# The guess for batch 2 taken out of the third attention, and two loads of v moved behind stores, in a kernel of attention and experts

## The chip, the cores and the metric

The kernel runs on one core of a Trainium2 chip, as one launch. The metric is the time of one execution on the device, in microseconds (us). Three runs of the kernel before took 358.21, 357.4 and 357.49 us; the median is 357.49. One further execution was recorded by the hardware profiler; all rows below come from it.

## The reference, cut to what matters

Eight batches; 16 query heads share 4 key heads; 384 tokens of 64 numbers per head. Each token's 16 heads side by side make a row of 1024, which goes to one of 16 experts (4 groups of 4).

```
scores = q @ k.T / sqrt(64);  attn = softmax(scores);  a = attn @ v        # per head
x = a.transpose(0, 2, 1, 3).reshape(3072, 1024)
g = argmax(x @ w_group);  e = argmax(x @ w_expert[g])                      # per token
out = softmax_g[g] * softmax_e[e] * (relu(x @ w1[g, e]) @ w2[g, e])
```

The kernel loads one expert per batch, chosen ahead of the gate by a guess from the mean of v, weights its output by what the gate really says, and has a loop at the end for tokens whose expert was not that one.

## The kernel before, in words

**Attention.** `Attn(b)` handles batch b in 24 units (`NU`), six to each pair of heads. For a unit TensorE makes a score (L318, four bf16 matmuls into a PSUM tile of the kind `s`, of which there are two), ScalarE its exp (L324) into one of 16 `e` tiles, and TensorE multiplies that by v (`pv`, L337, eight float32 matmul records into a tile of the kind `o`, two of them). `run` issues score u+2 ahead of pv u, then the unit's tail and whatever a table (`steps0`, `steps1`, `steps2`) puts there; a key such as 4.5 stands between pv 4 and the tail of unit 4. The sums of the exps are formed in pairs: GpSimd adds unit u to unit u-1 (`pair`, L345), then VectorE reduces the pair (`reduce`, L354). For a unit named in `apart` GpSimd adds nothing, and VectorE reduces both. `later` names units whose pair is called by hand, `lags` the unit at which a reduce is called. `join_keys` adds the parts, `sums` takes the total by four matmuls with a constant (L416) and VectorE's reciprocals (L432).

**Between two attentions.** `normalise` has VectorE spread the reciprocals (L455) and multiplies x by them (L459, on VectorE or GpSimd); `cast` writes x in bf16 (L464 on ScalarE, L466 on GpSimd). The block of batch b then computes the gate of batch b (`gate_logits`, L474, 64 matmul records) and the expert of batch b-1: `moe_h` (`ffn_h`, L636: four tiles of 16 matmuls) and `ffn_y` (L650, three chunks of 16), whose rows ScalarE or VectorE scales (`y_out`) and SP stores by two DMAs a chunk (L671).

**The guess.** The sum of v over the keys (`sum_v`: three GpSimd additions, L112 to L114; for batch 0 one VectorE reduce, L121) is halved and summed over partitions by a matmul of two columns (`guess_mean`, L480), copied by VectorE (L482), and multiplied with the gate's matrix (`guess_logits`, L487). For batch 2 this happens in units 1 and 2 of its own attention, followed by nine small VectorE instructions that pick the expert (`pick_guess`). The gate's tile of batch 1 is the same PSUM tile. For batch 3 the mean stands between the halves of the second chunk of `ffn_y`, for batches 4 to 7 (`ahead`) in front of the first chunk.

**Loads.** SP loads v in float32 (`load_v`, L105, two buffers), transposes k and q by DMA (L152, L153, L147) and stores the output, all in the order in which the code issues them. GpSimd issues the loads of k and q (L96, L101), which write bf16 into one buffer each, and of w1 and w2 (L546, L552), 2 MB each as written; the profile calls the queue of GpSimd's loads q0 and that of SP's DMAs q1. In `first_block` (behind the second attention) `load_v(3)` is issued first; in `block(2)` `load_v(4)`. `after_transposes` makes GpSimd wait until the DMA transposes of q are done (L604) before it fetches the weights. In `block(3)` the order on GpSimd is load_k(5), load_q(5), sum_v(4), that wait, the fetches, and the pairs of the fourth batch's attention.

Everything is issued in the order of the code on each engine; no planner moves it.

Of the kernel before, what the change touches and what calls it, by code (L numbers as in the profile page):

```python
# [10 lines left out]
BF16 = mybir.dt.bfloat16  # L11
# [7 lines left out]
def kernel(  # L19
# [48 lines left out]
    def ps_tile(which, shape=None, dtype=F32):  # L68
        if which == "x":
            which = f"o{1 - turn['o']}"  # L70
        else:
            turn[which] = 1 - turn[which]
            which += str(turn[which])
        return psum.tile(shape or [P, 2, 512], dtype, name="ps_" + which)
# [11 lines left out]
    def head_pair(m):  # L86

        g, r = m // 2, m % 2
        return KG * (2 * (g // 2) + r) + g % 2
# [13 lines left out]
    def load_v(b, src=None):  # L103
        vraw[b] = vpool.tile([P, NA, NC * D], F32, name="v_raw")
        nc.sync.dma_start(out=vraw[b], in_=rows(v[b] if src is None else src))  # L105
# [9 lines left out]
                             in1=s[:, :, 2 * D:])  # L115
        vsum[b] = t

    def first_sum_v():
        vsum[0] = gpool.tile([P, NA * D], BF16, name="vsum")
        with nc.allow_low_precision(reason="the guess of an expert alone reads this"):  # L120
            nc.vector.tensor_reduce(  # L121
                out=vsum[0].rearrange("p (a d) -> p a d", d=D),
                in_=vraw[0].rearrange("p a (c d) -> p a d c", d=D), axis=AX.X, op=ALU.add)

    def new_qT(b):
        qT[b] = xpool.tile([P, KQ * SC, P], BF16, name="qT")
# [282 lines left out]
                in_=red3[b][:, g:h, :parts[b][g]].rearrange("p g c t j -> p g (t j) c"),  # L409
                axis=AX.X, op=ALU.add)  # L410

    def sums(b, g0, g1, which, tiles=False):
        sm = ps_tile(which)[:, :, :(g1 - g0) * 2 * NB]
        for r in range(2):
            if not tiles:
                nc.tensor.matmul(out=sm[:, r], lhsT=half32[:, r, :],  # L416
                                 rhs=red[b][:, g0:g1].rearrange("p g t j -> p (g t j)"),
                                 start=True, stop=True)
                continue
            rs = slice(r * H2, (r + 1) * H2)  # L420
            for t in range(2):
                nc.tensor.matmul(
                    out=sm[t * D:(t + 1) * D, r].rearrange("p (g t j) -> p g t j", t=2, j=NB)[:, :, t],
                    lhsT=half32[rs, r, t * D:(t + 1) * D], rhs=red[b][rs, g0:g1, t],
                    start=True, stop=True)
        if b not in inv:
            inv[b] = gpool.tile([P, KQ, NB], F32, name="inv", bufs=2)
        iv = inv[b][:, 2 * g0:2 * g1].rearrange("p (g r) j -> p r g j", r=2)
        sm = sm.rearrange("p r (g t j) -> p r g t j", t=2, j=NB)
        for t in range(2):  # L430
            ts = slice(t * D, (t + 1) * D)
            nc.vector.reciprocal(out=iv[ts], in_=sm[ts, :, :, t])  # L432

    Q = P // 4

# [25 lines left out]
    def cast(b, m, eng=None):  # L461
        ks = slice(2 * m, 2 * m + 2)
        if eng is None:
            nc.scalar.copy(out=xb[b][:, ks, :], in_=xT[b][:, ks, :])  # L464
        else:
            eng.tensor_copy(out=xb[b][:, ks, :], in_=xT[b][:, ks, :])  # L466
# [3 lines left out]
    def gate_logits(b, pt):  # L470
        for m in range(KQ):
            x = xT[b][:, m, :].rearrange("p (j t x) -> p t j x", t=4, x=32)
            for t in range(4):
                nc.tensor.matmul(out=pt[32 * t:32 * t + 32, 0, :S // 4],  # L474
                                 lhsT=wg[:, head_pair(m), :], rhs=x[:, t],
                                 start=(m == 0), stop=(m == KQ - 1))

    def guess_mean(b, pt):
        pm = pt[:, 1, :2]
        nc.tensor.matmul(out=pm, lhsT=vsum[b], rhs=halfb, start=True, stop=True)  # L480
        vm = gpool.tile([P, 2], BF16, name="vm")
        nc.vector.tensor_copy(out=vm, in_=pm)  # L482
        return vm

    def guess_logits(vm, out_):
        for r in range(2):
            nc.tensor.matmul(out=out_, lhsT=vm[:, r:r + 1].to_broadcast([P, P]),  # L487
                             rhs=wg2[:, r, :], start=(r == 0), stop=(r == 1))
# [142 lines left out]

    def ffn_h(x, w1, hT, f0, which):
        h = ps_tile(which)
        for jj in range(2):
            for m in range(KQ):
                nc.tensor.matmul(out=h[:, jj, :S],  # L636
                                 lhsT=w1[:, head_pair(m), (f0 + jj) * P:(f0 + jj + 1) * P],
                                 rhs=x[:, m, :], start=(m == 0), stop=(m == KQ - 1))
        if f0 + 2 < FQ:
            nc.scalar.activation(hT[:, f0:f0 + 2, :], h[:, :, :S], ACT.Relu)  # L640
        else:
            for jj in range(2):
                nc.scalar.activation(hT[:, f0 + jj, :], h[:, jj, :S], ACT.Relu)  # L643
# [29 lines left out]
    def moe_y(b, c, which):  # L673
        y_out(b, c, ffn_y(w2s[b], hTs[b], c, which))

    def do(f, *a):
        return lambda: f(*a)
# [46 lines left out]
    def x_logits(b):  # L724
# [5 lines left out]
    index_constants()  # L730
    steps0 = {
        0: [gate_matrix_2],
        2: [do(first_q1, "x"), first_sum_v],
        4: [do(first_k, NC, 2 * NC, "x")],
        7: [do(x_mean, 0)],
        8: [do(x_logits, 0)],
# [21 lines left out]
    def first_fetch():  # L758
# [21 lines left out]
            lambda: mean(1, state["pt"]),  # L780
            do(at[1].pair, 7),
            do(at[1].reduce, 7),
            do(moe_h, 0, 2, "s"),
            do(at[1].pair, 13),
            do(at[1].pair, 15),
# [11 lines left out]
    at[1].run(steps1)  # L797

    def first_block():
        load_v(3)  # L800
        moe_y(0, 0, "s")
        sum_v(2)
        load_k(3)
        load_q(3)
        at[1].reduce(NU - 1)
        join_keys(1, 0, Hkv)
        y = ffn_y(w2s[0], hTs[0], 1, "s", (0,))
        sums(1, 0, Hkv, "o")
        ffn_y(w2s[0], hTs[0], 1, "s", (1,), y)
        y_out(0, 1, y)  # L810
        y = ps_tile("o")
        normalise(1, 0, "x")
        normalise(1, 2, "x")
        cast(1, 0)
        ffn_y(w2s[0], hTs[0], 2, "o", (0,), y)
        at[2] = Attn(2, later=(1,), lags={5: [1], 6: [3], **{u: [u - 2] for u in range(7, NU, 2)}})
        at[2].score(0)
        at[2].score(1)
        ffn_y(w2s[0], hTs[0], 2, "o", (1,), y)
        y_out(0, 2, y)  # L820
        normalise(1, 1, None, pool)
        normalise(1, 3, None, pool)

    def second_gate():
        gate_logits(1, state["pt"])
# [2 lines left out]
    first_block()  # L828
    before_attention(2)
    steps2 = {  # L830
        1: [do(cast, 1, 2), do(at[2].pair, 1), do(x_mean, 2)],
        2: [do(x_logits, 2)],
        3: [do(cast, 1, 1)],
        4.5: [second_gate],
        6: [do(cast, 1, 3)],
        8: [do(read_pick, 2)],
    }
    at[2].run(steps2)

# [2 lines left out]
    def block(b):  # L842
        last = b == B - 1
        f = b - 1
        early = b >= EARLY
        if b + 2 < B:
            load_v(b + 2)
        if not early:
            after_transposes(b + 1)
# [15 lines left out]
            pick_w2(b)  # L865
        moe_h(f, 0, "s")
        at[b].reduce(NU - 1)
        join_keys(b, 0, Hkv)
        if b == 2:
            gate_softmax(1, state["gl"], False)()  # L870
            out_weights(1)
# [15 lines left out]
        cast(b, 1)  # L887
        normalise(b, 3)
        moe_y(f, 0, "s")
        cast(b, 2)  # L890
        if not ahead:
            pt = ps_tile("o")
        y = ffn_y(w2s[f], hTs[f], 1, "s", (0,))
        if ahead:
            guess_logits(vm, guess_out(pt))
        elif not last:
            vm = guess_mean(b + 1, pt)
        ffn_y(w2s[f], hTs[f], 1, "s", (1,), y)
        y_out(f, 1, y)
        gate_logits(b, pt)  # L900
        if not (last or ahead):
            guess_logits(vm, guess_out(pt))
        if b <= EARLY:
            at[b + 1] = Attn(b + 1)
            at[b + 1].start()
        cast(b, 3)
        w = gate_softmax(b, gate_rows(pt, not last), not last)
        if not last:
# [165 lines left out]
```

## Time and profile before

| | |
|---|---|
| median of three runs | 357.49 us (357.4 to 358.21) |
| the profiled execution | 356.7 us, of which the instructions span 354.9 |
| TensorE busy | 345.9 us, 97% of the span |
| VectorE, ScalarE, GpSimd busy | 72%, 63%, 62% |
| TensorE's granted clock | 0.996 of full speed over the span |
| DMA | 67.15 MB as written: 41.03 on GpSimd's queue (67.2% of 16 engines), 24.94 on SP's (30.4%) |
| the third attention (batch 2): its unit 0 starts at | 72.98 us |
| the block of batch 2 starts at | 95.04 us |
| the fourth attention (batch 3) starts at | 118.78 us |
| the block of batch 3 starts at | 137.96 us |
| the fifth attention (batch 4) starts at | 160.91 us |

Busy time is read per engine; matmuls are pipelined, so TensorE's is not its work at its peak. A line of the timeline joins neighbouring instructions of one kind, and a bracket at its end says how long the engine stood idle before it and what released it.

### The profile page before, as it was taken

The page shows a single profiled execution, that of the slowest core. Times are in us where ns is not written, and L with a number is a line of the kernel's source. Part 1 is how long each engine was busy: PE and PEld are TensorE (multiplying, and loading weights), DVE is VectorE, ACT ScalarE, POOL GpSimd, SP SyncE. Part 2 cuts the span into 40 slices and gives each one's busy share as a digit, 9 for nine tenths or more (in the row PEclk, how much of TensorE's full clock was granted, in tenths as well). Part 3 has the DMA queues.
Part 4 walks back from the last instruction along what each step waited for, and adds up shares of the span by engine and source line. Part 5 has one row for each costly group of instructions (what it writes and reads, how often), then busy time and mean ns, then how long its engine had stood idle before and what let it go on. Part 6 is the DMA issues. An engine that isn't in the chain of part 4 may idle for free.

```text
span 354.9 us, 9208 instructions
## 1 busy us (share of the span) xinstructions
PE 345.9 (97%) x3801; PEld 182.5 (51%) x3816; DVE 253.9 (72%) x520; ACT 225.0 (63%) x296; POOL 220.2 (62%) x171
## 2 busy tenths in 40 slices
PE   8999999999999999999999999999999999999994
PEld 4455565445555455554555555545545545555642
DVE  5797769767697777976689667886769677796031
ACT  5899925299536795378954499355982669444311
POOL 7889985869935499308991299804995059900000
PEclk9999999999999999999999999999999999999998
DMA  8979999799989999999999999999995995099925
GB/s 199 215 135 188 220 207 160 134 275 222 193 174 176 258 209 182 206 163 203 229 221 207 193 220 211 218 192 193 228 211 95 197 263 130 2 175 219 258 48 137
DMA packets 69327, 67.15 MB, mean 189 GB/s; under 512 B 37113, under 2 KB 49401, under 8 KB 69281
## 3 DMA queue, kind: packets, MB, share of 16 engines
q0 software_dynamic: 26640, 41.03, 67.2%
q1 hardware_dynamic: 42272, 24.94, 30.4%
q8 instruction: 32, 0.52, 0.6%
q10 hardware_dynamic: 368, 0.54, 0.4%
q14 instruction: 15, 0.11, 0.1%
HBM read 86.07 MB, written 12.58 MB: 278 GB/s over the span
## 4 chain that ended last, share of the span: by engine, by line
PE 87%; ACT 4%; POOL 3%; DVE 2%; issue 1%; DMA 1%; ACTq 0%; SPq 0%; POOLq 0%; DVEq 0%
PE ps_o L337 30%; PE ps_s L636 22%; PE ps_s L650 13%; PE ps_s L318 8%; PE ps_o L650 6%; PE ps_o L474 3%; ACT e L324 2%; POOL w L345 2%; PE ps_o L636 1%; PE ps_s L951 1%; PE ps_o L951 1%; DMA w<-in_q_dram 1%; POOL xb L466 1%; ACT w L324 0%; DVE inv L432 0%
## 5 line engine op out<-in xcount | busy, mean ns | idle before, releaser
L345 POOL TENSOR_TENSOR e<-e 128x768 f32<-128x768 f32 x91 | 162.8, 1826 | 37.0 <-PE ps_s L318 30.8
L324 ACT ACTIVATE e<-ps_s 128x768 f32<-128x768 f32 x187 | 147.7, 813 | 15.0 <-PE ps_s L318 12.8
L337 PE MATMUL ps_o<-e,v_raw 64*64 64x384 f32 x1496 | 150.1, 482 | 0.0
L354 DVE TRANSPOSE_TENSOR_REDUCE red<-e 128x24 f32<-128x768 f32 x95 | 91.4, 972 | 36.7 <-POOL e L345 36.6
L636 PE MATMUL ps_s<-xb,w 128*128 128x384 bf16 x480 | 80.1, 326 | 0.1
L337 PEld LDWEIGHTS ps_o<-e,v_raw 64*64 64x64 f32 x1496 | 55.3, 133 | 35.7 <-issue 29.5
L636 PEld LDWEIGHTS <-w 128*128 128x128 bf16 x512 | 49.4, 98 | 36.4 <-issue 4.5
L318 PE MATMUL ps_s<-qT,kT 64*64 64x384 bf16 x768 | 65.0, 325 | 0.4
L650 PEld LDWEIGHTS <-hT 128*128 128x128 bf16 x336 | 31.5, 98 | 37.7 <-issue 1.5
L650 PE MATMUL ps_s<-w,hT 128*128 128x512 bf16 x217 | 49.5, 379 | 0.4
L640 ACT ACTIVATE hT<-ps_s 128x768 bf16<-128x768 f32 x23 | 18.6, 810 | 46.7 <-PE ps_s L636 43.3
L318 PEld LDWEIGHTS <-kT 64*64 64x64 bf16 x768 | 24.5, 105 | 35.6 <-issue 33.6
L669 ACT ACTIVATE ot<-ps_s,we 128x1024 f32<-128x1024 f32 x14 | 15.6, 1115 | 19.0 <-PE ps_s L650 17.2
L604 POOL COPY tok<-qT 1x1 bf16<-1x1 bf16 x6 | 1.1, 179 | 42.5 <-DMA qT<-q_raw 42.5
L379 DVE COPY xT<-ps_o 128x768 f32<-128x768 f32 x26 | 24.0, 924 | 2.7 <-ACT xb L464 1.5
L455 DVE STREAM_TRANSPOSE e<-inv 128x768 f32<-128x768 f32 x26 | 25.2, 971 | 0.2
L464 ACT CAST xb<-xT 128x768 bf16<-128x768 f32 x28 | 23.1, 830 | 3.4 <-DVE xT L459 3.2
L650 PE MATMUL ps_o<-w,hT 128*128 128x512 bf16 x105 | 24.0, 379 | 1.1 <-issue 1.1
L459 DVE TENSOR_TENSOR xT<-xT,e 128x768 f32<-128x768 f32 x24 | 23.1, 962 | 0.8
L495 DVE STREAM_TRANSPOSE gl<-ps_o 128x96 f32<-128x96 f32 x8 | 2.3, 283 | 18.7 <-PE ps_o L474 15.0
L643 ACT ACTIVATE hT<-ps_s 128x384 bf16<-128x384 f32 x14 | 6.1, 488 | 12.5 <-PE ps_o L480 7.2
L474 PEld LDWEIGHTS ps_o<-xT,wg 128*32 128x32 f32 x448 | 9.2, 110 | 3.3 <-issue 2.1
(140 smaller groups left out, 233.3 us busy)
## 6 DMA issues: line engine op xcount, KB each, us to landing
w<-in_moe_w_dram POOLq DMA_DIRECT2D x16, 2048.0 KB, 21.9
out_dram<-ot SPq DMA_DIRECT2D x42, 256.0 KB, 6.9
q_raw<-in_q_dram POOLq DMA_DIRECT2D x7, 768.0 KB, 11.0
v_raw<-in_v_dram SPq DMA_DIRECT2D x7, 384.0 KB, 5.7
k_raw<-in_k_dram POOLq DMA_DIRECT2D x7, 192.0 KB, 6.4
out_dram<-ot SPq DMA_DIRECT2D x10, 128.0 KB, 2.4
w<-in_q_dram POOLq DMA_DIRECT2D x3, 192.0 KB, 6.3
w<-in_k_dram SPq DMA_DIRECT2D x2, 192.0 KB, 3.7
```

The costliest lines, as they stand in the source:

```text
L318: nc.tensor.matmul(out=sT[r * H2:(r + 1) * H2, s, :S], lhsT=kT[b][s * D:(s + 1) * D, key_block(b, s, g // 2, c), ks], rhs=qT[b][s * D:(s + ...
L324: nc.scalar.activation(e.rearrange("p t (s x) -> p s t x", s=2), sT[:, :, :S].rearrange("p s (t x) -> p s t x", t=2), ACT.Exp, scale=scale)
L337: nc.tensor.matmul(out=oT[t * D:(t + 1) * D, r, :S], lhsT=vraw[b][r * H2:(r + 1) * H2, g // 2, c * D:(c + 1) * D], rhs=self.e[u][r * H2:(r ...
L345: nc.gpsimd.tensor_add(out=self.e[u - 1], in0=self.e[u - 1], in1=self.e[u])
L354: nc.vector.tensor_reduce(out=red3[b][:, g, parts[b][g]].rearrange("p t j -> p (t j)"), in_=self.e[w].rearrange("p t (j x) -> p (t j) x", ...
L379: nc.vector.tensor_copy(out=dst, in_=src)
L455: nc.vector.transpose(out=rb.rearrange("p k (j x) -> p k j x", x=32), in_=inv[b][:, ks].unsqueeze(3).to_broadcast([P, 2, NB, 32]))
L459: eng.tensor_mul(out=x, in0=x, in1=rb)
L464: nc.scalar.copy(out=xb[b][:, ks, :], in_=xT[b][:, ks, :])
L474: nc.tensor.matmul(out=pt[32 * t:32 * t + 32, 0, :S // 4], lhsT=wg[:, head_pair(m), :], rhs=x[:, t], start=(m == 0), stop=(m == KQ - 1))
L636: nc.tensor.matmul(out=h[:, jj, :S], lhsT=w1[:, head_pair(m), (f0 + jj) * P:(f0 + jj + 1) * P], rhs=x[:, m, :], start=(m == 0), stop=(m == ...
L650: nc.tensor.matmul(out=y[:, nh, :], lhsT=hT[:, f, c * P:(c + 1) * P], rhs=w2[:, f, nh * HALF:(nh + 1) * HALF], start=(f == 0), stop=(f == ...
```

## The change

- `first_sum_v` becomes `reduce_v(b)`, which also makes the sum of v of batch 2, on VectorE, in the steps at unit 17 of the second attention, behind `reduce(7)`. The three GpSimd additions for batch 2 in `first_block` go.
- The guess of batch 2: its mean is made in `sums(1)` of `first_block`, by one matmul behind those of the sums, into a free part of the same tile, and copied behind the reciprocals. Its logits and the pick stand at unit 1 of the third attention (before: mean at 1, logits at 2).
- In the third attention units 0 and 1 are summed by VectorE (`apart=(1,)`), both reduces at unit 2; `join_keys` of its first heads stands at unit 10.
- The casts of batch 1 (slices 2, 1, 3), before at units 1, 3 and 6, stand together at 4.5, behind the gate of batch 1.
- `load_v(3)` is issued behind `moe_y(0, 0)`, `load_v(4)` behind `moe_y(1, 0)`; each then follows two stores on SP.
- In the block of batch 2 the mean for batch 3 stands behind the gate, its logits behind the first two scores of the next attention.
- `ffn_h` takes its first tile in two passes, first the slices 0 to 5 of x for both halves, then the slices 6 and 7.

```diff
-    def first_sum_v():
+    def reduce_v(b):
...
-    def sums(b, g0, g1, which, tiles=False):
-        sm = ps_tile(which)[:, :, :(g1 - g0) * 2 * NB]
+    def sums(b, g0, g1, which, tiles=False, mean=None):
+        pt = ps_tile(which)
+        sm = pt[:, :, :(g1 - g0) * 2 * NB]
...
+        if mean is not None:
+            guess_product(mean, pt, MEAN)
...
+        return pt if mean is None else guess_copy(pt, MEAN)
...
+    MEAN = 2 * KQ * NB
+
+    def guess_product(b, pt, n):
+        nc.tensor.matmul(out=pt[:, 1, n:n + 2], lhsT=vsum[b], rhs=halfb, start=True, stop=True)
+
+    def guess_copy(pt, n):
+        vm = gpool.tile([P, 2], BF16, name="vm")
+        nc.vector.tensor_copy(out=vm, in_=pt[:, 1, n:n + 2])
+        return vm
...
     def ffn_h(x, w1, hT, f0, which):
         h = ps_tile(which)
-        for jj in range(2):
-            for m in range(KQ):
...
+        ends = [0, KQ] if f0 else [0, KQ - 2, KQ]
+        for m0, m1 in zip(ends, ends[1:]):
+            for jj in range(2):
+                for m in range(m0, m1):
...
             do(at[1].reduce, 7),
+            do(reduce_v, 2),
             do(moe_h, 0, 2, "s"),
...
     def first_block():
+        moe_y(0, 0, "s")
         load_v(3)
-        moe_y(0, 0, "s")
-        sum_v(2)
...
-        sums(1, 0, Hkv, "o")
+        state["vm"] = sums(1, 0, Hkv, "o", mean=2)
...
-        at[2] = Attn(2, later=(1,), lags={5: [1], 6: [3], **{u: [u - 2] for u in range(7, NU, 2)}})
+        at[2] = Attn(2, apart=(1,), lags={6: [3], **{u: [u - 2] for u in range(7, NU, 2)}})
...
     steps2 = {
-        1: [do(cast, 1, 2), do(at[2].pair, 1), do(x_mean, 2)],
-        2: [do(x_logits, 2)],
-        3: [do(cast, 1, 1)],
-        4.5: [second_gate],
-        6: [do(cast, 1, 3)],
+        1: [second_logits],
+        2: [do(at[2].reduce, 1)],
+        4.5: [second_gate, do(cast, 1, 2), do(cast, 1, 1), do(cast, 1, 3)],
         8: [do(read_pick, 2)],
+        10: [do(join_keys, 2, 0, 1)],
     }
...
-        if b + 2 < B:
+        if early and b + 2 < B:
             load_v(b + 2)
...
         moe_y(f, 0, "s")
+        if not early:
+            load_v(b + 2)
         cast(b, 2)
...
-        elif not last:
-            vm = guess_mean(b + 1, pt)
         ffn_y(w2s[f], hTs[f], 1, "s", (1,), y)
         y_out(f, 1, y)
         gate_logits(b, pt)
         if not (last or ahead):
-            guess_logits(vm, guess_out(pt))
+            vm = guess_mean(b + 1, pt)
         if b <= EARLY:
             at[b + 1] = Attn(b + 1)
             at[b + 1].start()
+        if not (last or ahead):
+            guess_logits(vm, guess_out(pt))
```

## Rows read from the trace of the kernel before

**Rows 1.** The page, busy us of each engine (share of the span) and instructions.

```profile
PE 345.9 (97%) x3801; PEld 182.5 (51%) x3816; DVE 253.9 (72%) x520; ACT 225.0 (63%) x296; POOL 220.2 (62%) x171
```

**Rows 2.** Chain of waits, third attention: start us, us, what.

```profile
74.20 0.71 ACT e L324
...
81.64 0.72 ACT xb L464
```

**Rows 3.** Timeline, TensorE, third attention: start us, us, line, operation, tiles, count.

```profile
74.95 0.36 PE L318 MATMUL ps_s<-qT,kT 64*64 64x384 bf16 x4
...
83.12 0.36 PE L318 MATMUL ps_s<-qT,kT 64*64 64x384 bf16 x4
...
83.93 0.36 PE L318 MATMUL ps_s<-qT,kT 64*64 64x384 bf16 x4
```

**Rows 4.** Timeline, TensorE, second attention from unit 17.

```profile
44.29 3.01 PE L636 MATMUL ps_s<-xb,w 128*128 128x384 bf16 x16
...
48.73 2.76 PE L636 MATMUL ps_s<-xb,w 128*128 128x384 bf16 x16
```

**Rows 5.** Timeline, GpSimd (POOL), the last cast of batch 0.

```profile
44.64 0.83 POOL L466 CAST xb<-w 128x768 bf16<-128x768 f32 x1 [0.51 <-DVE w L459]
```

**Rows 6.** The v sum of batch 0 (L121): min, median, max ns, first and last start.

```profile
L121 DVE TENSOR_REDUCE vsum<-v_raw x1: 1519/1519/1519, 11.3 to 11.3; 128x128 bf16<-128x768 f32 x1
```

**Rows 7.** Timeline, VectorE, second attention from unit 17.

```profile
48.91 0.16 DVE L482 CAST vm<-ps_o 128x2 bf16<-128x2 f32 x1 [1.73 <-PE ps_o L480]
48.99 0.97 DVE L354 TRANSPOSE_TENSOR_REDUCE red<-e 128x24 f32<-128x768 f32 x1
51.57 0.28 DVE L495 STREAM_TRANSPOSE gl<-ps_o 128x96 f32<-128x96 f32 x1 [1.62 <-PE ps_o L487]
```

**Rows 8.** DMA issues, 66 to 71 us: count, KB, us to landing.

```profile
q_raw<-in_q_dram POOLq DMA_DIRECT2D x1, 768.0 KB, 29.5
```

**Rows 9.** Timeline, ScalarE, third attention.

```profile
74.10 1.50 ACT L324 ACTIVATE e<-ps_s 128x768 f32<-128x768 f32 x2
```

**Rows 10.** Timeline, SP's queue: start us, us, line, what it issues.

```profile
66.35 8.98 SPq L671 DMA_DIRECT2D out_dram<-ot  x6
...
102.08 0.53 SPq L105 DMA_DIRECT2D v_raw<-in_v_dram  x1
110.94 4.68 SPq L671 DMA_DIRECT2D out_dram<-ot  x4
```

**Rows 11.** DMA queues, 61 to 66 us: packets, MB, share of 16 engines.

```profile
q1 hardware_dynamic: 274, 0.39, 24.5%
```

**Rows 12.** DMA queues, 82 to 91 us.

```profile
q0 software_dynamic: 927, 1.89, 111.4%
```

**Rows 13.** DMA queues, 71 to 82 us.

```profile
q0 software_dynamic: 692, 1.39, 68.6%
q1 hardware_dynamic: 479, 1.57, 38.8%
```

**Rows 14.** Timeline, GpSimd, blocks of batches 2 and 3.

```profile
103.85 0.18 POOL L604 COPY tok<-qT 1x1 bf16<-1x1 bf16 x1 [5.01 <-DMA qT<-q_raw]
...
106.27 1.53 POOL L112 TENSOR_TENSOR vs<-v_raw 128x384 f32<-128x384 f32 x1
...
143.54 0.89 POOL L101 DMA_DIRECT2D q_raw<-in_q_dram  x1 [1.50 <-DMA qT<-q_raw]
144.45 1.01 POOL L112 TENSOR_TENSOR vs<-v_raw 128x384 f32<-128x384 f32 x1
...
146.09 0.47 POOL L114 TENSOR_TENSOR vsum<-vs 128x128 bf16<-128x128 f32 x1
```

**Rows 15.** Timeline, TensorE, block of batch 3: the guess's mean for batch 4.

```profile
148.37 0.17 PE L480 MATMUL ps_o<-halfb,vsum 128*128 128x2 bf16 x1
```

**Rows 16.** Timeline, TensorE, block of batch 4: the gate.

```profile
197.90 1.53 PE L474 MATMUL ps_o<-xT,wg 128*32 128x96 f32 x64
```

**Rows 17.** Timeline, VectorE, block of batch 4: the last multiplication of x.

```profile
196.16 0.96 DVE L459 TENSOR_TENSOR xT<-xT,e 128x768 f32<-128x768 f32 x1
```

More of the change, by code (lines that the diff above doesn't have):

```diff
@@ L116, in sum_v @@
         vsum[b] = t
-    def first_sum_v():
-        vsum[0] = gpool.tile([P, NA * D], BF16, name="vsum")
+    def reduce_v(b):
+        vsum[b] = gpool.tile([P, NA * D], BF16, name="vsum")
         with nc.allow_low_precision(reason="the guess of an expert alone reads this"):
             nc.vector.tensor_reduce(
-                out=vsum[0].rearrange("p (a d) -> p a d", d=D),
-                in_=vraw[0].rearrange("p a (c d) -> p a d c", d=D), axis=AX.X, op=ALU.add)
+                out=vsum[b].rearrange("p (a d) -> p a d", d=D),
+                in_=vraw[b].rearrange("p a (c d) -> p a d c", d=D), axis=AX.X, op=ALU.add)
     def new_qT(b):
@@ L476, in gate_logits @@
                                  start=(m == 0), stop=(m == KQ - 1))
-    def guess_mean(b, pt):
[L479 to L483, printed above, removed]
+    MEAN = 2 * KQ * NB
[5 more added lines that the diff above has]
+        return vm
+    def guess_mean(b, pt):
+        guess_product(b, pt, 0)
+        return guess_copy(pt, 0)
     def guess_logits(vm, out_):
@@ L633, in ffn_h @@
         h = ps_tile(which)
-        for jj in range(2):
-            for m in range(KQ):
-                nc.tensor.matmul(out=h[:, jj, :S],
-                                 lhsT=w1[:, head_pair(m), (f0 + jj) * P:(f0 + jj + 1) * P],
-                                 rhs=x[:, m, :], start=(m == 0), stop=(m == KQ - 1))
+        ends = [0, KQ] if f0 else [0, KQ - 2, KQ]
+        for m0, m1 in zip(ends, ends[1:]):
+            for jj in range(2):
+                for m in range(m0, m1):
+                    nc.tensor.matmul(out=h[:, jj, :S],
+                                     lhsT=w1[:, head_pair(m), (f0 + jj) * P:(f0 + jj + 1) * P],
+                                     rhs=x[:, m, :], start=(m == 0), stop=(m == KQ - 1))
         if f0 + 2 < FQ:
@@ L732 @@
         0: [gate_matrix_2],
-        2: [do(first_q1, "x"), first_sum_v],
+        2: [do(first_q1, "x"), do(reduce_v, 0)],
         4: [do(first_k, NC, 2 * NC, "x")],
@@ L822, in first_block, with second_logits @@
         normalise(1, 3, None, pool)
+    def second_logits():
+        state["pt"] = ps_tile("x")
+        x_logits(2)
     def second_gate():
@@ L867, in block @@
         at[b].reduce(NU - 1)
-        join_keys(b, 0, Hkv)
+        join_keys(b, int(b == 2), Hkv)
         if b == 2:
```

## The prediction

> **What bounds the kernel now.** I read the page first: TensorE is busy for 97% of the span [rows 1], so the time is TensorE's work plus its few waits, and an edit pays only where it moves one of these. The chain of waits, read in order of time, is TensorE nearly throughout and leaves it at few places; the change touches two. In the first ten units of the third attention the chain runs over ScalarE's exps and over a cast between them [rows 2]. TensorE's timeline shows what that costs: scores of neighbouring units stand 0.81 us apart where nothing waits, but 8.2 us lie between the score at 74.95 and that at 83.12, of which seven units and the gate product of 1.5 us need 7.2 [rows 3, 16]. In the second attention the first product of an expert takes 3.01 us for 16 matmuls [rows 4], because its last slice of x is cast on GpSimd until 45.47 [rows 5]. Then I read the DMA by windows and the queues of SP and GpSimd, since half of the change moves loads. The reader is to see there that v3 and v4 (v of batches 3 and 4) now travel in stretches with nothing else to move, and that the weights of an expert, with k and q behind them, fill the engines for some 30 us without a gap.
>
> **The parts.**
>
> *Product split over the last two slices (ffn_h).* Without the split, six matmuls run and the seventh waits for the cast; with it twelve run first, at 0.16 to 0.17 us each (2.76 us over 16) from 44.29 to about 46.3. The cast ends at 45.47. So the wait goes: 3.01 less 2.76 for the undisturbed 16 is **0.25 us** [rows 4, 5]. For the later batches x is cast long before; nothing is gained or lost.
>
> *reduce_v(2) on VectorE.* The one such instruction in the trace takes 1.52 us [rows 6]. It stands behind a reduce that begins at 48.99 and takes 0.97, so it ends at about 51.5; the next work, the gate's transpose, begins at 51.57 because it waits for TensorE [rows 7]. It is covered to within 0.1 us; if the cover is gone, the softmax and what hangs on it come up to 0.2 us later. The three GpSimd additions that go stood before k and q loads that wait in line behind weights, so their going moves nothing: q would be issued some 2.1 us earlier (as long as the three take for batch 4, from 144.45 to 146.56 [rows 14]), but it now takes 29.5 us to land, behind the weights [rows 8].
>
> *The guess's mean behind sums(1), its logits at unit 1.* TensorE's two-column product is listed with 0.17 us [rows 15], of which its successor may hide nearly all; VectorE's copy with 0.16 [rows 7]. Both lie in front of VectorE's normalise, on which ScalarE's cast and all its exps wait, so the exps start 0.1 to 0.35 later for the two, 0.25 earlier for the split: I take no shift (from -0.15 to +0.1).
>
> *Casts of batch 1 out of the units, three in a row after the gate.* Call T the start of exp 2, now 74.10. An exp takes 0.70 and a cast 0.72 (the chain lists 0.71 and 0.72) [rows 2, 9]. Score 4 needs exp 2's buffer and comes at T+0.85 as now. From there: three units to T+3.3, the gate to T+4.8, score 9 ready at T+6.4. ScalarE: exps 2 to 6 to T+3.5, three casts to T+5.66, exp 7 to T+6.36, so score 9 at T+6.46 and score 11 at T+8.1, where it now is at T+9.0 [rows 3]. **Gain 0.95 us**, the 0.25 above included, between 0.8 and 1.2. The gate's product no longer meets the nine small VectorE steps of the pick, which come one unit earlier.
>
> *Pair 1 summed by VectorE.* GpSimd loses one addition, VectorE gains one reduce of 0.97 [rows 7] and a small join. VectorE has the room at unit 2, in front of the gate. Without it GpSimd's last pair would hold up sums(2), which TensorE reaches 0.95 us sooner; so I give this edit nothing of its own: it keeps the 0.95, and up to that much would be lost without it. In the block after it the mean moves behind the gate and the logits behind two scores: four instructions in a new order, -0.05 to +0.15 us, taken as nothing.
>
> *The loads of v3 and v4.* v4 is issued at 102.08 now, ahead of the weights; afterwards each stands behind the first two stores of its block, v3 at about 67 and v4 at about 111 [rows 10]. Alone, v3 uses 24.5% of the 5 us in which it now travels, 1.22 us of all 16 engines [rows 11]; v4 has the same bytes. At the new places the weights' queue is in the middle of its train. What a transfer beside it costs: alone the train moves 1.89 MB in 9 us, 0.21 MB/us [rows 12]; beside 1.57 MB of stores it moves 1.39 MB in 11 us, where 2.31 would have gone: 0.92 MB or 4.4 us lost, 2.8 us per MB [rows 13]. For 0.39 MB that is 1.1 us; by the packet (256 of v against 384 of those stores) 2.9. I take v's own busy time, **1.2 us each**, bounds 1.1 and 2.9. The Trainium skill (DMA: Bandwidth & Descriptors, "Issuing engines are not separate DMA queues") says that transfers from all issuing engines run on the same 16 DMA engines and interleave, which speaks against this edit; the trace agrees, with 1.39 MB in place of 2.31 [rows 13]. By that page's limit of 358 GB/s (Specifications), an estimate for 0.39 MB is 1.1 us, and the sum below would be 0.2 us smaller.
>
> Both delays add up along one line. v3 delays k and q of batch 3, hence their transposes, for which GpSimd already waits 5 us before it fetches weights [rows 14]; the weights start 1.2 later, v4 goes into them, and q of batch 4 is 2.4 later. Its transposes hold GpSimd at 143.54, in front of load_q(5) (1.50 us idle), and the v sum of batch 4 is queued behind that load and ends at 146.56 [rows 14]. TensorE takes it up at 148.37 [rows 15]. The slack is 148.37 - 146.56, less some 0.06 for the signal: **1.75 us**. With 2.4 later it is gone, and TensorE has nothing it may pass ahead. What waits behind the mean is all of the block's second product.
>
> One more term: the v sum's first addition takes 1.01 us at 144.45 but 1.53 at 106.27, beside VectorE's multiplications [rows 14]. Moved 2.4 us, to 146.9 and on, the sum's 2.1 us fall in with those of batch 3: between nothing and half as much again, 1.1; I take **0.7**, nearer to the slow row, since most of the sum falls there. The Trainium skill (GPSIMD Engine Reference, "Key points") names VectorE instructions with two SBUF inputs as what GpSimd contends with; the 1.53 beside such multiplications agrees, and by the rule what runs before the first of them would be spared, which gives 0.4 in place of 0.7 and a sum 0.3 us smaller.
>
> **Sum.** A stall here eats what was won before it: with TensorE 0.95 earlier the stall is 0.95 longer. So the end moves by 2.4 + 0.7 - 1.75 = **+1.35 us**, whatever the gain in the attention is. Next comes block 4: GpSimd's pairs of batch 4 also start 2.4 later (they wait for transposes that hang on load_q(5)), and the last multiplication, which ends at 197.12, has until about 199.0, when the gate at 197.90 reaches its slices [rows 16, 17]: 1.9 + 1.35 - 2.4 leaves 0.85, no second stall. The profiled execution took 356.7 (span 354.9), so 358.05; it lies 0.8 below the median of the runs, 357.49, which becomes **358.8**. Bounds: 2.2 - 1.75 = +0.4 below; above, 2 x 1.7 by a middle price per packet, 1.1, and up to 1.2 from k of batch 5, which GpSimd now issues while q's transposes run: some +3 if two of these three come true, to 360.5.
>
> **Rivals.** *The loads are hidden and the gain is kept.* The moved loads could use time that the train leaves, as it begins (first packets are slow in both trains) or because q's transposes gain what v4 gave up. For it: v is 0.39 MB against 6 MB of train. Against it: the train's queue shows above 100% of the engines where it is alone [rows 12]. It decides if both together delay q of batch 4 by less than 0.8 us: then 357.49 - 0.95 = 356.5 (356.2 to 356.8), faster. *The burst of casts takes the gain back.* Three casts hold ScalarE 2.2 us while it has 0.1 us a unit to spare; if exp 7 comes 0.9 later than computed, and the loads are hidden or hit the slack just so, nothing is left: 357.5 (357.1 to 357.8). Against it speaks that the gate's 1.5 us, in which no score asks for ScalarE, lies under them. *A second stall.* If each v costs 1.7 us or more, or k of batch 5 slows the transposes, the mean is 2 to 4 us late and block 4 or the fetch of the next weights waits as well: 361.5 (360.5 to 362.5). That the guess would not leave the attention can't be: its product and copy are placed in sums by the code.
>
> **How the numbers follow.** Less than 0.3%, 1.07 us, can't be told from no change here. Forecast 0.50 (357.9 to 360.5; 0.38 slower, 0.12 same); loads hidden 0.30 (half faster, half same, since 0.95 lies near the line); gain taken back 0.08 (same); second stall 0.12 (slower). Faster 0.15, same 0.35, slower 0.50. The range, 356.4 to 360.6, leaves out the lower third of the hidden case and most of the second stall.
>
> **What would show it.** Right: the v loads' packets beside the weights; GpSimd's wait for q's transposes (now 5.01 us before the fetch) about 1.2 longer, and that before load_q(5) 2.4 to 3.5 longer; TensorE waiting about 2 us for the two-column product of batch 4; scores 4 to 11 of the third attention about 8.1 - 0.85 = 7.2 us apart. Wrong: no wait at that product, or q of batch 4 landing as before; then the time lies below 357. If the ten units keep their 8.2 us, the cast step was wrong, which the sum would hide.

## The result, and the profile after

The changed kernel takes **362.53 us** (median, 362.14 to 363.63) against 357.54 (357.40 to 358.21) for the kernel before: ratio 1.0141, interval 1.0120 to 1.0162. The forecast was 358.8, with a range to 360.6. The change makes the kernel slower, at the place forecast and by nearly four times the size forecast. The profiled executions took 363.63 (span 362.0) and 356.7 (span 354.9).

The page, busy us of each engine (share of the span) and instructions, against [rows 1]:

```profile
PE 347.9 (96%) x3801; PEld 183.6 (51%) x3816; DVE 255.9 (71%) x523; ACT 224.9 (62%) x296; POOL 215.8 (60%) x167
```

Work hardly changed; TensorE waits more. First what the change was to win. TensorE's timeline after (start us, us, line, operation, tiles, count), against [rows 3, 4]:

```profile
44.29 2.77 PE L649 MATMUL ps_s<-xb,w 128*128 128x384 bf16 x16
...
74.86 0.36 PE L318 MATMUL ps_s<-qT,kT 64*64 64x384 bf16 x4
...
82.31 0.36 PE L318 MATMUL ps_s<-qT,kT 64*64 64x384 bf16 x4
```

The split product takes 2.77 in place of 3.01. Scores 4 and 11 of the third attention stand 7.45 us apart in place of 8.17 (the prediction said about 7.2). ScalarE's timeline shows the three casts in a row and the exps behind them:

```profile
77.65 2.29 ACT L468 CAST xb<-xT 128x768 bf16<-128x768 f32 x3
79.84 4.56 ACT L324 ACTIVATE e<-ps_s 128x768 f32<-128x768 f32 x6
```

So the attention's gain is there. It is lost at one product in the block of batch 3; TensorE's timeline again, against [rows 15, 16]:

```profile
152.70 0.19 PE L485 MATMUL ps_o<-halfb,vsum 128*128 128x2 bf16 x1 [5.26 <-POOL vsum L114]
...
153.56 7.25 PE L663 MATMUL ps_s<-w,hT 128*128 128x512 bf16 x22 [0.22 <-issue]
160.65 0.20 PE L498 MATMUL ps_o<-wg,vm 128*128 128x20 bf16 x2
...
197.93 5.34 PE L663 MATMUL ps_s<-w,hT 128*128 128x512 bf16 x23
203.11 0.20 PE L498 MATMUL ps_o<-wg,vm 128*128 128x20 bf16 x2
204.98 1.27 PE L478 MATMUL ps_o<-xT,wg 128*32 128x96 f32 x50
```

(The view ends at 206 us and cuts the last line off.) TensorE waits 5.26 us for the v sum. The product comes 4.33 later than before (152.70 against 148.37), so 0.93 had been won by then. The gate of batch 4 is 7.08 later (204.98 against 197.90), and so is all that follows. The 2.75 between the two is the clock: behind the wait the same product takes 7.25 us for 22 matmuls where the next block takes 5.34 for 23. TensorE's busy time and granted clock in that stretch (window; us; busy of PE, PEld, DVE, ACT, POOL; clock; DMA share; GB/s):

```profile
147.40:152.70 5.30, 0.04 (x1) 0.00 (x1) 1.85 (x3) 2.42 (x4) 2.79 (x4) 0.88 0.90 217
152.70:156.00 3.30, 3.08 (x8) 1.22 (x10) 3.01 (x5) 0.00 (x0) 0.00 (x0) 0.50 1.31 151
156.00:160.00 4.00, 4.00 (x14) 1.57 (x13) 0.84 (x1) 0.88 (x1) 0.00 (x0) 0.71 1.31 150
```

TensorE stood idle for 5.3 us, and the work behind it ran at a granted clock of 0.50 (1.2 in place of 2.4 GHz) until about 158. Of the five executions the profiled one has the lowest mean clock (0.987, the others 0.991 to 0.995) and the longest time, 1.1 us above the median.

**Where the v sum's delay comes from.** SP's queue after (start us, us, line, what it issues), against [rows 10]:

```profile
67.41 0.62 SPq L105 DMA_DIRECT2D v_raw<-in_v_dram  x1
...
99.47 4.12 SPq L147 DMA_TRANSPOSE qT<-q_raw  x1
...
111.07 0.64 SPq L105 DMA_DIRECT2D v_raw<-in_v_dram  x1
...
141.88 3.69 SPq L147 DMA_TRANSPOSE qT<-q_raw  x1
```

and the same two transposes before:

```profile
98.29 3.69 SPq L147 DMA_TRANSPOSE qT<-q_raw  x1
...
137.41 4.24 SPq L147 DMA_TRANSPOSE qT<-q_raw  x1
```

GpSimd's timeline after, against [rows 14]:

```profile
106.64 0.23 POOL L615 COPY tok<-qT 1x1 bf16<-1x1 bf16 x1 [9.64 <-DMA qT<-q_raw]
...
144.10 0.74 POOL L96 DMA_DIRECT2D k_raw<-in_k_dram  x1 [3.82 <-DMA kT<-k_raw]
149.67 0.89 POOL L101 DMA_DIRECT2D q_raw<-in_q_dram  x1 [4.84 <-DMA qT<-q_raw]
150.58 1.00 POOL L112 TENSOR_TENSOR vs<-v_raw 128x384 f32<-128x384 f32 x1
151.67 0.45 POOL L113 TENSOR_TENSOR vs<-vs 128x128 f32<-128x128 f32 x1
152.19 0.45 POOL L114 TENSOR_TENSOR vsum<-vs 128x128 bf16<-128x128 f32 x1
```

Read down these rows, the delay grows at four places:

| step | before | after | later by | new here |
|---|---|---|---|---|
| q(3)'s transposes issued | 98.29 | 99.47 | 1.18 | 1.18: v3 beside the train |
| GpSimd sees them done | 103.85 | 106.64 | 2.79 | 1.61 |
| q(4)'s transposes issued | 137.41 | 141.88 | 4.47 | 1.68: v4 beside the train |
| load_q(5), which waits for them | 143.54 | 149.67 | 6.13 | 1.66 |
| v sum of batch 4 ends | 146.56 | 152.64 | 6.08 | none |

The two terms of v are the ones forecast (of the 1.18, 0.27 is there in e1 below too, where no load is moved). The two of 1.6 are not: the transposes take longer from issue to landing. The DMA view gives that time as the last column. Before, 98 to 104 us, then 137 to 146 us:

```profile
qT<-q_raw SPq DMA_TRANSPOSE x1, 5.5
```

```profile
qT<-q_raw SPq DMA_TRANSPOSE x1, 5.6
```

After, 99 to 105 us (queues first: packets, MB, share of 16 engines), then 141 to 149 us:

```profile
q8 instruction: 1, 0.02, 1.0%
q14 instruction: 1, 0.01, 0.3%
...
qT<-q_raw SPq DMA_TRANSPOSE x1, 7.1
```

```profile
qT<-q_raw SPq DMA_TRANSPOSE x1, 7.2
```

In the first window after, two instruction loads fall beside q(3)'s transposes: 16 KB on queue q8, at 104.6, and 8 KB on q14, at 102.1. Before, both come behind them, at 104.6 to 105.2. In the second window load_k(5) falls beside q(4)'s: it waits 3.82 us for k(4)'s transposes and is issued 2.22 us after q(4)'s. Before, it came straight behind GpSimd's pairs, 3.90 us after q(4)'s, and its first packets (142.7) behind their last (142.5):

```profile
141.31 0.74 POOL L96 DMA_DIRECT2D k_raw<-in_k_dram  x1
```

The experiments tell which of these matter.

### The profile page after: what moved, and what is told of

Same layout as the page of the kernel before. It is cut to its first block, busy times and chain, and to the rows that moved or that the text cites. A ratio compares the mean times of both kernels' runs of the same rounds, so it can differ in the third digit from the quotient of the medians.

```text
span 362.0 us, 9207 instructions
## 1 busy us (share of the span) xinstructions
PE 347.9 (96%) x3801; PEld 183.6 (51%) x3816; DVE 255.9 (71%) x523; ACT 224.9 (62%) x296; POOL 215.8 (60%) x167
## 4 chain that ended last, share of the span: by engine, by line
PE 75%; DMA 11%; issue 5%; POOL 3%; ACT 3%; DVE 1%; ACTq 0%; SPq 0%; POOLq 0%; DVEq 0%
PE ps_o L337 27%; PE ps_s L649 16%; PE ps_s L663 12%; DMA q_raw<-in_q_dram 8%; PE ps_s L318 8%; PE ps_o L663 5%; PE ps_o L478 3%; DMA qT<-q_raw 2%; ACT e L324 2%; PE ps_o L649 1%; PE ps_s L969 1%; POOL e L345 1%; PE ps_o L969 1%; DMA w<-in_q_dram 1%; POOL vs L112 1%
## 5 line engine op out<-in xcount | busy, mean ns | idle before, releaser
L345 POOL TENSOR_TENSOR e<-e 128x768 f32<-128x768 f32 x90 | 160.9, 1816 | 33.9 <-PE ps_s L318 30.7
L354 DVE TRANSPOSE_TENSOR_REDUCE red<-e 128x24 f32<-128x768 f32 x96 | 92.4, 972 | 36.6 <-POOL e L345 36.3
L663 PE MATMUL ps_s<-w,hT 128*128 128x512 bf16 x217 | 52.0, 393 | 0.5 <-issue 0.2
```

Source lines behind the costliest of these rows:

```text
L345: nc.gpsimd.tensor_add(out=self.e[u - 1], in0=self.e[u - 1], in1=self.e[u])
L354: nc.vector.tensor_reduce(out=red3[b][:, g, parts[b][g]].rearrange("p t j -> p (t j)"), in_=self.e[w].rearrange("p t (j x) -> p (t j) x", ...
L663: nc.tensor.matmul(out=y[:, nh, :], lhsT=hT[:, f, c * P:(c + 1) * P], rhs=w2[:, f, nh * HALF:(nh + 1) * HALF], start=(f == 0), stop=(f == ...
```

## The experiments

Theory at first: the two v loads cost it all, and the rest of the change is a gain. Rival: the rest costs something too. Ratios are against runs of the kernel before on the same chip.

**e1: both v loads back at their old places.**

```
 def first_block():                       # and load_v(b + 2) first in every block
+    load_v(3)
     moe_y(0, 0, "s")
-    load_v(3)
```

> The changed kernel with both v loads at their former places, all else kept. Theory (the moved loads delay q of batch 4, and TensorE waits for the v sum of batch 4): the wait of 5.3 us in front of the two-column product is gone, the 1.1 us won up to there stays, so 356.4 us (0.997 of before). Rival (the stall comes from the new order of the guesses and sums): it stays near 361 to 362.5.

Measured: 360.95, ratio 1.0094 (1.0061 to 1.0128). The theory falls: without any moved load 3.6 us are lost. The time of its runs goes with the mean granted clock: three at 0.995 to 1.000 took 359.27 to 359.63, four at 0.988 to 0.994 took 360.95 to 362.29. So the chain near full clock costs some 2 us here, and the rest goes with the clock. The rows are of the run at 359.44. Its GpSimd rows show the same chain, without the delay of v (trans_q(3) is issued at 98.56):

```profile
105.84 0.18 POOL L615 COPY tok<-qT 1x1 bf16<-1x1 bf16 x1 [8.53 <-DMA qT<-q_raw]
...
147.57 0.89 POOL L101 DMA_DIRECT2D q_raw<-in_q_dram  x1 [5.36 <-DMA qT<-q_raw]
```

**e2, e3: only v3, or only v4, moved.** The changed kernel with load_v(4), or load_v(3), back.

> The changed kernel with v of batch 4 back at its former place, v of batch 3 left behind the stores. Theory: the v sum of batch 4 ends some 2 to 3 us later than before (1.3 for the load, up to 1.5 for what the transposes of q then collide with); with 0.75 us of slack left TensorE waits 1 to 2.3 us: 357.5 to 359. Rival (the delays do not add, one load alone makes the whole stall): 361 or more here or in the next kernel.

> The changed kernel with v of batch 3 back, v of batch 4 left behind the stores. Theory: q of batch 4 lands some 1.6 us later, its transposes up to 1.7 later again, TensorE waits 1 to 2.5 us: 357.3 to 359. Rival (one load alone makes the whole stall): 361 or more.

Measured: 361.97 (1.0081 to 1.0153) and 362.64 (1.0104 to 1.0183). Both miss the same way: the base they were added to was 360.95, not 356.4. TensorE waits 3.88 and 4.01 us at the product, e1's 3.49 with little on top, and the intervals overlap.

**e4: the kernel before with only the two v loads moved.**

> The kernel before with only the two v loads moved. Theory: q of batch 4 is 3 to 6 us late, of which 1.75 us are slack, and the mean for batch 3, which here still stands inside the second chunk, waits 1 us for its own v sum: 359.5 to 362.5. Rival (the loads alone are hidden, the stall needs the rest of the change): 357.5.

Measured: 362.08, 1.0121 (1.0076 to 1.0165), as expected. So the loads alone cost it all as well: either half of the change is enough, and the halves don't add. What they share is that q(3)'s transposes land late (105.84 in e1, 107.05 here).

**e5: e1 with the v sum ahead of load_k and load_q on GpSimd.**

```
+if not last: sum_v(b + 1)
 if b + 2 < B: load_k(b + 2); load_q(b + 2)
-if not last: sum_v(b + 1)
```

> The changed kernel with both v loads back and, in block 3 and later, the v sum issued on GpSimd in front of the loads of k and q (before: behind them). Theory (the stall is GpSimd's order: the v sum stands behind load_q(5), which waits for the transposes of q): the sum ends at about 142.5, TensorE does not wait for the two-column product, k of batch 5 is issued behind the transposes instead of beside them, and the pairs of batch 4 start soon enough: 356.4 us. Rival (the transposes themselves are late whatever GpSimd does, and the loss comes back as a late start of the pairs of batch 4): no wait at the product but one of 2 to 4 us at the gate of block 4, 358 to 360.

Measured: 358.73, 1.0071 (1.0030 to 1.0111). Seven of its twelve runs took 357.8 to 358.8 and five 363.0 to 364.6; the trace is of one at 357.76, and none shows what the five lose. In it TensorE no longer waits at the product, so GpSimd's order is the link between q(4)'s transposes and TensorE. Two waits of 0.4 and 0.3 us for weights follow, at 190.8 and 233.3; q(3)'s transposes are as late as in e1 (seen at 106.00). But q(4)'s now land in 5.5 us: load_k(5) is issued 3.25 us after them (142.96 against 139.71), in e1 1.98.

**e6: e1 with pair 1 summed on GpSimd again.**

```
-at[2] = Attn(2, apart=(1,), lags={6: [3], ...})
+at[2] = Attn(2, later=(1,), lags={5: [1], 6: [3], ...})
-1: [second_logits],  2: [do(at[2].reduce, 1)],
+1: [do(at[2].pair, 1), second_logits],
```

> The changed kernel with both v loads back and the first pair of the third attention added by GpSimd as before. Theory (a block that starts 1 us earlier brings two instruction loads into the tail of the transposes of q of batch 3, which costs them 2 us): GpSimd's pairs end at 98.8 again, the block is where it was, the instruction loads come near 104.9 and the transposes end near 103.6: 357 to 357.5, faster than e1 although the third attention gains less. Rival (collision by chance, not by position): as e1, 360 to 361.

Measured: 357.13, 0.9997 (0.9981 to 1.0013). Its TensorE row shows the gain given back at the sums of batch 2:

```profile
100.35 0.69 PE L417 MATMUL ps_o<-red,half 128*128 128x96 f32 x4 [0.75 <-DVE red L407]
```

Behind the sums TensorE is back at its old time (100.35 against 100.42), q8 loads at 104.7, the transposes land in 5.5 us, and nothing is lost. So e1's loss comes with its gain: there TensorE passes the sums 0.7 us sooner (99.72), and its load comes 1 us sooner.

**e7: e1 with the casts spread over units 1, 3 and 6 as before.**

> The changed kernel with both v loads back and the casts of batch 1 at units 1, 3 and 6 again. TensorE's scores 4 to 11 take 8.0 us or more instead of 7.4, so 0.7 us of the 1.1 are lost. Theory (position of the instruction loads against the transposes): with the block only 0.3 us earlier than before the collision is rarer, 357 to 359, faster than e1. Rival (the casts are pure gain): 0.7 us slower than e1, 361.6.

Measured: 361.30 (1.0075 to 1.0148), a miss: the burst of casts is not what matters. The loads come at 103.6 and 103.8 as in e1, and GpSimd sees the transposes at 105.86. TensorE passes the sums at 100.07, only 0.35 us sooner than before, and that is enough.

**e8: the changed kernel with 24 products of 512 columns ahead of the two-column product,** to keep TensorE busy in its wait (they write nothing that is used).

> The changed kernel with 24 matmuls of 512 columns (some 5.2 us, results overwritten) in front of the two-column product of batch 4, so that TensorE works through its wait; nothing else differs. Theory (after the wait of 5.3 us the granted clock is 0.5 for some 5 us, which costs 2.7 us in the profiled execution): no drop of the clock in the block of batch 3, 360 to 362 and less spread over runs. Rival (the clock costs nothing beside the wait): 362.5 as changed.

Measured: 362.85 (1.0116 to 1.0188). The clock stays at 1.00 and TensorE's work behind the wait runs at its normal pace, but the time is the same. Its rows show why: gate of batch 3 at 160.41, 4.97 later than before (155.44), gate of batch 4 at 204.52, 6.62 later than [rows 16]:

```profile
160.41 1.53 PE L478 MATMUL ps_o<-xT,wg 128*32 128x96 f32 x64
...
204.52 1.54 PE L478 MATMUL ps_o<-xT,wg 128*32 128x96 f32 x64
```

So TensorE loses 1.65 us one block on in place of the clock; 1.1 of it are waits for VectorE, whose reduces wait for GpSimd's pairs. GpSimd is late there because q(5)'s transposes are. The 24 products moved TensorE's instruction loads too: one of 16 KB now falls on the end of this set (166.7). The set is issued 1.5 us later than in the changed kernel (161.60 against 160.12) and lands in 7.2 us in place of 5.5, and GpSimd sees it at 168.83 in place of 165.62:

```profile
168.83 0.18 POOL L615 COPY tok<-qT 1x1 bf16<-1x1 bf16 x1 [15.56 <-DMA qT<-q_raw]
```

So e8 doesn't settle what the low clock costs: it took the clock away and brought a new late landing.

**e9 and e10: the same work, with TensorE's instruction count shifted.** The kernel warms TensorE up with nine dummy products. In e9 (on e1) they become 5 large and 46 small ones, in e10 (on the **kernel before**) 6 large and 14 small: 42 and 11 more instructions at the start, nothing else.

```
-for i, n in enumerate((4, 4, 4, 4, 4, 4, 4, 1, 1)): matmul(warm[..n * P], ...)
+for i in range(6):  matmul(warm[:, i % 2, :], ...)
+for i in range(14): matmul(warm[:, i % 2, :32], lhsT=onesb, rhs=onesb[:, :32])
```

> The kernel before, with one large warm-up product at the start replaced by 14 small ones: 11 more TensorE instructions, nothing else. Theory: the q8 load that now comes at 104.8, just behind q(3)'s transposes (done 103.6), comes about 1.8 us earlier, near 103.0, and hits their tail: GpSimd sees them at 105 to 106 instead of 103.85, load_q(5) goes from 143.5 to 145.5-147.5, TensorE waits 0.5 to 2.5 us at batch 4's two-column product, and the time is 357.8 to 360. Rival: the load's place doesn't matter, 357.3 as before.

Measured: **359.65, 1.0063 (1.0049 to 1.0077)**: 2.2 us lost to eleven small products that hide in a wait. The transposes are issued at 98.36, as before, but the DMA view of 98 to 104 us now has the load in it:

```profile
q8 instruction: 1, 0.02, 1.0%
...
qT<-q_raw SPq DMA_TRANSPOSE x1, 7.2
```

```profile
105.58 0.18 POOL L607 COPY tok<-qT 1x1 bf16<-1x1 bf16 x1 [6.43 <-DMA qT<-q_raw]
```

TensorE pays in three waits of 2.1 us together (waits: total, times, longest), none of which stands in the list of the kernel before:

```profile
PE ps_s L653 <- DMA w<-in_moe_w_dram: 1.2, 1, 1.2
PE ps_o L483 <- POOL vsum L114: 0.6, 1, 0.6
PE ps_o L477 <- DVE vm L485: 0.3, 1, 0.3
```

The data are not slower. The packets of under 512 B, nearly all the transposes' own, are through at 103.3 before and at 103.5 in e10 (DMA view, 98.0 to 103.3 and 98.0 to 103.5):

```profile
DMA packets 4318, 1.09 MB, mean 205 GB/s; under 512 B 4315, under 2 KB 4318, under 8 KB 4318
```

```profile
DMA packets 4357, 1.11 MB, mean 202 GB/s; under 512 B 4342, under 2 KB 4357, under 8 KB 4357
```

Only the landing is late. From 103.5 to 104.1 the load's one packet holds 10.1% of 16 engines, 0.97 us of a single one:

```profile
q8 instruction: 1, 0.02, 10.1%
```

> The kernel of e1 (changed kernel, both v loads back), with two of the large warm-up products at the very start replaced by 46 small ones: 42 more TensorE instructions, the same work otherwise. Theory: the 16 KB instruction loads (queue q8, 32 in the span, one for about 120 products) belong to TensorE's program, so each comes 42 products earlier, about 7 us where a product of the expert takes 0.17 us; the one that hit q(3)'s transposes at 103.8 in e1 comes near 96.7. Then GpSimd sees the transposes at 103.9 to 104.6 instead of 105.8, load_q(5) is issued at 143.5 to 145 instead of 147.6, TensorE waits less than 1 us at batch 4's two-column product, and the time is 356.4 to 357.6. Rivals: the small q14 load (8 KB, still near 103.6) does the harm, or engines' contention does: then all is as in e1, 360 to 361.

Measured: 360.13, 1.0069 (1.0049 to 1.0088): a partial miss. The q8 load came at 97.2, so it belongs to TensorE's instructions (q14 stayed, 104.4, so that one does not). But there it met k(3)'s transposes: SP's second one took 1.95 us in place of 1.29 to 1.30, and q(3)'s were issued at 99.33. With q14 alone behind them they landed in 6.4 us:

```profile
qT<-q_raw SPq DMA_TRANSPOSE x1, 6.4
```

So the landing takes 5.5 us without a load at the tail, 6.4 with the 8 KB one, and 7.1 to 7.2 with the 16 KB one there, wherever the 8 KB one fell (102.1 in the changed kernel, 103.5 in e1, 104.7 in e10).

**e11, e12: k and q of the next batch between w1 and w2 of the train,** on e1 and on the changed kernel.

```
 after_transposes(b + 1)
 pick_w1(b)
+load_k(b + 2); load_q(b + 2)
 pick_w2(b)
 sum_v(b + 1)
-load_k(b + 2); load_q(b + 2)
```

> The kernel of e1, with k and q of batches 3 and 4 issued between w1 and w2 of the train instead of behind both. Theory: the transposes of q(3) and q(4) run some 8 us earlier, beside w2, and are done before the instruction loads at 103.6 and before load_k(5); GpSimd no longer waits for them, the weights of batch 2 start several us earlier, load_q(5) is issued by 143, TensorE waits under 0.3 us at batch 4's two-column product, and the gain of the third attention is kept: 356.0 to 356.8. Rival: transposes beside the weights take so much longer that they end as late as now, and the time stays at 359 to 361; or w2 comes late and TensorE waits for it in front of the expert's second product (above 358).

Measured: **356.59, 0.9978 (0.9968 to 0.9988)**, faster than both kernels. The time is as expected, the way there only in part. The transposes are issued earlier but beside w2 they take 11.1 to 11.7 us, so GpSimd sees q(3)'s at 105.88, no sooner than in e1. q(4)'s, however, are issued at 133.64 and done in time:

```profile
145.24 0.89 POOL L101 DMA_DIRECT2D q_raw<-in_q_dram  x1 [1.88 <-DMA qT<-q_raw]
```

```profile
148.30 0.18 PE L485 MATMUL ps_o<-halfb,vsum 128*128 128x2 bf16 x1 [0.17 <-POOL vsum L114]
```

> The changed kernel itself (both v loads behind the stores) with the same new order w1, k, q, w2. Theory: with the transposes some 8 us earlier, the 1.2 to 1.6 us that each v costs the train lie in slack: 356.2 to 357.2. Rival: the v loads beside the train cost what they cost in any order, 1.3 and 1.65 us, and come back at some later wait: 358 to 361.

Measured: 362.30, 1.0144 (1.0124 to 1.0164), a miss, and the rival's case: the v loads still delay the transposes (GpSimd sees q(3)'s at 107.30), load_q(5) is issued at 147.66, and TensorE waits 3.81 us.

**e13: e1 with load_k(5) held until q(4)'s transposes are done.**

```
 if b + 2 < B:
+    if b == 3: after_transposes(b + 1)
     load_k(b + 2)
```

> The kernel of e1, with GpSimd waiting for all of q(4)'s transposes before it issues load_k(5). Theory: k(5), which e1 issues at 141.5 beside them, lengthens them; alone they take 5.6 us from their issue, as q(3)'s do in the kernel before (98.29 to 103.85), in place of 8.1 (139.5 to 147.6). So load_q(5) is issued at 145.8 to 146.3 although k goes in front of it, TensorE's wait at batch 4's two-column product falls from 3.5 to 1.8-2.4 us, and the time to 358.8 to 360. Rival: they are lengthened by the stores and v5, which stay, and load_k(5) is only later: load_q(5) at 148 or more, 361 to 362.5.

Measured: 360.82, 1.0075 (1.0048 to 1.0102). Right on the transposes: q(4)'s land in 5.5 us, against 7.5 in e1 (DMA views from 139 and 139 to 146 us):

```profile
qT<-q_raw SPq DMA_TRANSPOSE x1, 5.5
```

```profile
qT<-q_raw SPq DMA_TRANSPOSE x1, 7.5
```

Again the packets end at the same time in both (4297 small ones by 144.9 here, 4322 by 144.7 in e1). Wrong on the time: k now stands in front of q, and the v sum falls beside VectorE's work:

```profile
146.80 0.89 POOL L101 DMA_DIRECT2D q_raw<-in_q_dram  x1
147.71 1.61 POOL L112 TENSOR_TENSOR vs<-v_raw 128x384 f32<-128x384 f32 x1
149.40 1.26 POOL L113 TENSOR_TENSOR vs<-vs 128x128 f32<-128x128 f32 x1
```

The sum takes 3.5 us in place of e1's 2.7, and TensorE still waits 3.07.

**e14: e1 with one 32-bit product in place of the nine of the warm-up,** to move q8's load later.

> The kernel of e1, with TensorE's nine warm-up products at the start replaced by one of 32-bit type over the same ones: 5 to 8 fewer TensorE instructions pairs, the rest the same. Theory: the q8 load of 103.8 comes 0.8 to 1.2 us later, 104.6 to 105.0, when q(3)'s transposes are all but done; q14 still hits them. GpSimd sees them at 104.2 to 105.1 in place of 105.84, load_q(5) is issued 1 to 2.5 us earlier than in e1 (145 to 146.6), the wait at batch 4's product is 1 to 2.5 in place of 3.5, and the time 358 to 360, apart from what the shorter warm-up costs in the first 10 us, which is read from the first scores. Rival: q14 alone does the harm: 105.8 and 361 as in e1.

Measured: 361.85 (1.0103 to 1.0186), and nothing settled. All of the kernel began later (trans_q(3) at 100.54 against 98.56), the load moved with it to 105.7, 5.2 us behind the issue as in e1, and the transposes took 7.2 again. This is no accident of e14. In all eleven runs whose set of q(3) met a 16 KB load (the changed kernel, e1 to e5, e7, e8, e10, e13, e14) the load's packet stands within 0.3 us of the last 0.1 us in which the set still moves 20 packets, though that end lies anywhere from 103.4 to 105.5, and the set lands 2.0 to 2.2 us behind the packet (2.9 in e8). So a load asked for while the transposes run may be held until they end, and not meet their end by chance. No run shows when a load is asked for, so this is argued and not shown.

**e15: e11 with the v sum ahead of load_k and load_q in the blocks from 3 on.**

> The kernel of e11 with the v sum of the next batch ahead of load_k and load_q in the blocks from 3 on. Theory: e11 has 0.2 us of wait left at batch 4's product; this takes it away and starts k and q of batch 5 two us later, which has slack here: 356.2 to 356.7, not to be told from e11 (356.6). Rival: the later k and q of batch 5 cost later, as in e5 (stalls of 0.5 to 1.2): 357 to 358.

Measured: 358.05, 1.0024 (1.0003 to 1.0045). The rival was right: with no wait left to remove, later loads of batch 5 only cost.

## Why the prediction was wrong

*Right.* The place: TensorE waits at batch 4's two-column product, because the v sum stands behind load_q(5) on GpSimd. The slack of 1.75: the sum ended 6.08 later and the product began 4.33 later. The split (0.24 for 0.25). The cast step (0.81 at score 11, 0.93 by that product, for 0.95). v's price, nearly: 1.18 and 1.68 for 1.2 each.

*Wrong, and most of the miss: "q of batch 4 is 2.4 later".* The sum took the landing of each set of transposes as fixed and moved only their issue. Load_q(5) came 6.13 later: 2.86 by the v loads and 3.27 by two landings that grew from 5.5 to 7.1 and from 5.6 to 7.2. With 6.13 for 2.4, and nothing for the 0.7 below, the prediction's own sum gives the 4.33 by which the product came late. The first landing grew because the delay carried the tail of q(3)'s transposes onto the 16 KB instruction load that had come just behind it. e10 shows that this alone costs the kernel before 2.2 us. The Trainium skill (Runtime: NRT & Kernel Launch, "Instruction fetch mechanics") says that crossing a 16 KiB boundary of instructions costs one bump of a DMA queue's tail, mostly hidden. Here it was not hidden: 2.2 us were paid, through another transfer's landing, and the measurement decides. The second grew because load_k(5), no longer held back by GpSimd's pairs until q(4)'s transposes were nearly done, fell beside them; e13 shows the 2.0 us of it in e1, and e5 the same. The prediction had this outside its sum, as "up to 1.2 from k of batch 5", one of three mishaps of which two were allowed, and as a condition of its second stall.

*Wrong: "so the end moves by +1.35, whatever the gain in the attention is".* The gain alone, with no load moved, costs 3.6 us (e1; 2.0 to 2.3 in its runs near full clock), and without it the change costs nothing (e6). TensorE passes the sums of batch 2 0.7 us sooner, its instruction load comes 1 us sooner, and that is the end of the same transposes. Hence also "I give this edit nothing of its own" of VectorE's pair: the pair is what delivers the gain to the block, and in this kernel the collision with it.

*Wrong: the slower v sum, 0.7.* It took 2.1 us as before. That it can happen is shown by e13's 3.5.

*Not foreseen: the clock,* 2.75 us in the profiled execution. What it adds to the median is open: the rows' 4.33 for the late chain leave 0.66 of the median's 4.99, and e8 doesn't tell. In e1 and e13 the runs at 0.995 or more are some 2 us shorter than the rest (359.0 to 359.6 against 360.8 to 363.3).

Of the rivals the second stall came nearest (361.5): its condition, k of batch 5 slowing the transposes, was met. But no second stall made the time: TensorE's list of waits has no other new one for an engine or a transfer. "The loads are hidden" fell with e4.

*Left open.* Which engine q14's load serves; whether a load is held until the transposes end; and why a landing comes 1.7 us late when the packet beside it takes 0.97: the trace has no engine number for a packet. Both e10 and e13 changed the time of what they tested, and e10 nothing else of the work, but no run took the loads away altogether.

## What to carry to other kernels

A stage that ends "just in time" on a DMA landing has a margin that the busy shares don't show: look at what lies beside it and in the next microsecond or two on any queue, instruction loads included, before adding up delays. A chain of landings, each gating the next transfer in an in-order queue, multiplies a delay, here from 1.18 to 6.13 us in four steps. So give an edit that moves work sooner the same question as one that moves it later, and put the transfers that others hang on ahead in the queue (e11) before spending slack; with the v loads beside the train even that was not enough (e12).

## What the runs showed of the hardware

- The landing of a set of q's transposes depends on what comes beside its last packets: 5.5 to 5.6 us with nothing (before, e6), 6.4 with an 8 KB instruction load (e9), 7.1 to 7.2 with a 16 KB one (the changed kernel, e1, e4, e10; 7.7 in e2, 7.9 in e8), 7.2 to 7.5 with another load's first packets (the changed kernel, e1). In e10 against before, and e1 against e13, the packets themselves end within 0.2 us of each other.
- TensorE's program is loaded in 16 KB pieces, 32 in this span, one for about 119 products (3801 by 32); 42 more products at the start moved one from 103.8 to 97.2 (e1, e9). Eleven dummy products at the start moved one of them from 104.6 or later to about 103.5 and cost 2.2 us (e10).
- Transposes beside a weights' train take twice as long: 11.1 to 11.7 us in e11, against 5.5.
- Behind a wait of 5.26 us TensorE's granted clock was 0.50 (1.2 GHz) for 3.3 us and 0.71 on the mean over the next 4; kept at work through that wait, in e8, it was 1.00.
